# Staging the first feed-forward's results in the attention output's buffer, and a written order for ScalarE and VectorE in two of its four blocks

## Chip, cores and metric

One core of one Trainium2 chip. The metric is the device time of one execution in microseconds (us), and lower is better. The kernel before takes 912.31 us, the median of three runs (911.75 to 914.02).

## The reference, cut to what matters

```python
def reference(**kwargs):
    attn_out = _attn_ref(...)            # banded local attention plus 32 global tokens, 4 x 8 heads of 64
    B, H, S, D = attn_out.shape          # 4, 8, 544, 64
    x = attn_out.transpose(0, 2, 1, 3).reshape(B * S, H * D)     # 2176 tokens x 512
    x = _moe_ref(x, w_in, w_out)         # elu(x @ w_in) @ w_out, width 2048
    return _moe2_ref(x, w_gate, w_val, w_out, rms_g)
    # rms norm; silu(xn @ w_gate) * (xn @ w_val) @ w_out, width 1536
```

The weights arrive as 64-bit floats and are decoded on the chip to 32-bit ones with integer instructions. Every product of two 32-bit numbers is made of three passes over a high and a low part.

## The kernel before, in words

**First half, to about 500 us.** The 2048 local tokens go through the first feed-forward in four blocks of 512, called b=0 to b=3 here as in the code (so the change's "blocks 2 and 3" are b=1 and b=2). A block has 16 turns j. In a turn TensorE makes one `mm1` (12 matmuls L132 into `h`), then `mm2` of the turn before (12 matmuls L146 into the four accumulators `y0` to `y3`, in two halves), and between them pieces of the attention of block b+1: scores (L220, L226) at turns 0, 4, 8, 12, transposes (`ptp`, L244) one turn later, the product with v (`o`, L257) after the `mm1` of the turn after that. At turn 15 the attention's output `x` is transposed into `xT` for the next block (L280 to L282). The last `mm2` of a block comes in turn 0 of the next one, and `store_y` (L152 to L160) then evicts `y0` to `y3`, two on ScalarE and two on VectorE, and sends them to `yT` in DRAM with four DMAs of 256 KB.

Between `mm1` and `mm2` stands the elu: ScalarE `e<-h` (L121), ScalarE exp (L122), VectorE `e<-e,h` (L123), ScalarE `g<-e` (L139), VectorE low part `g<-e,g` (L140). The `e` tiles have two buffers, and two of the four eviction tiles `yev` take the same two; the other two take the two buffers `stg`.

**Weight decoding beside it.** In b=0 the first feed-forward's own weights are decoded; from turn 13 of b=0 on, through b=1 and b=2, the second one's (24 tasks: 18 decodings and 6 sums). A decoding is ScalarE |raw| (L83), four VectorE instructions (L90 to L93), then DMAs of the result to DRAM (`wS`, `wT`) and the load of the next 1 MB of raw weights into the raw buffer that came free. There are two raw buffers and two `dx` buffers. The sums (`w2_sums`, L483 to L486) are made in the raw buffer itself, so the load after them waits for their eight DMAs. SyncE issues all DMAs, in its own order.

TensorE's order is written out by hand throughout. ScalarE's and VectorE's is written by hand only in the first stretch of the kernel; in the rest a scheduler that plans with its own times chooses it. Tile pools hand out buffers by tag: a new tile of a tag waits until the readers of the one before it are done, DMAs among them. The tag `x32` has one buffer; the attention output `x` uses it from turn 2 to turn 15 of each block, in b=3 the global attention's `xg32`, and later a block of `yT` that is read back.

**Second half.** At turns 10 to 15 of b=3 the global tokens' first feed-forward runs beside the block; its result `yg` is copied (`ysb`, a `stg` tile), transposed (L721), evicted and stored. Then the second feed-forward's products follow: pairs of `product` (L732) into `A` and `Q`, ScalarE copies of `A` (L921, L936, L942), VectorE sums, and the second matmul `o` (L738), with ScalarE and VectorE splitting the weights (L586, L587) and squaring the next tokens (L609, L614) beside it.

Of the kernel before, what the change touches and what calls it, by code (L numbers as in the profile page):

```python
# [7 lines left out]
F32 = mybir.dt.float32  # L8
F32R = mybir.dt.float32r
# [3 lines left out]
AF = mybir.ActivationFunctionType  # L13
ALU = mybir.AluOpType
# [7 lines left out]
P = 128  # L22
# [6 lines left out]
HI_MIN = 2.0 ** -15  # L29
HI_MAX = 122880.0 - 2.0 ** -7  # L30
# [3 lines left out]
def f(ap):  # L34
    return ap.bitcast(F32)


def i32(ap):
    return ap.bitcast(I32)
# [3 lines left out]
def fused_kernel(ctx: ExitStack, tc: tile.TileContext, kq, vl, gkq, gv, w_in, w_out, w_gate, w_val, w_o2, rms_g, consts, out):  # L43
    nc = tc.nc
# [5 lines left out]
    stg = ctx.enter_context(tc.tile_pool(name="stg", bufs=2))  # L50
# [85 lines left out]
    def act1(h, n, fn=None):  # L136
        e = (fn or elu)(h, n)
        g = moe.tile([P, 2, 512], F32R, tag="g", name="g", bufs=2)
        nc.scalar.copy(g[:, 0, :n], e[:, :n])  # L139
        nc.vector.tensor_tensor(out=g[:, 1, :n], in0=e[:, :n], in1=f(g[:, 0, :n]), op=ALU.subtract)  # L140
        return g
# [8 lines left out]
        return [yps.tile([P, 512], F32, tag=f"y{i}", name=f"y{i}") for i in range(4)]  # L150

    def store_y(ys, t0, n):  # L152
        for dc in range(4):
            if dc % 2:
                t = moe.tile([P, 512], F32, tag="e", name="yev", bufs=2)
                nc.vector.tensor_copy(t[:, :n], ys[dc][:, :n])
            else:
                t = stg.tile([P, 512], F32, tag="stg", name="yev")
                nc.scalar.copy(t[:, :n], ys[dc][:, :n])
            nc.sync.dma_start(out=yT[:, dc, t0:t0 + n], in_=t[:, :n])  # L160


    SETS = ("A11", "A12", "S2", "S1", "S3", "A22", "S4")
# [14 lines left out]
    with ExitStack() as ls:  # L178
# [282 lines left out]
        def w2_decode(i):  # L461
            kind, c, G = order2[i]
            raw = raws2.pop(0)
            t = dec_abs(dec["t"], raw, keep=True)
            dec_bits(t, raw)
            t2 = t.rearrange("p (a n) -> p a n", a=2)
            if kind == "o":
                nc.sync.dma_start(out=wT[c:c + 2].rearrange("a p n -> p a n"), in_=t2)
                w2_load()
            elif c == 0:  # L470
                put(kind, G, "A11", t2[:, :, 0:256])
                held["a"] = t2
                w2_load()
            else:
                put(kind, G, "A12", t2[:, :, 0:256])
                put(kind, G, "A22", t2[:, :, 256:512])
                held["b"], held["raw"] = t2, raw

        def w2_sums(kind, G):
# [4 lines left out]
            nc.vector.tensor_tensor(out=s2, in0=s1, in1=t[:, :, 0:256], op=ALU.subtract)  # L484
            nc.vector.tensor_tensor(out=s3, in0=t[:, :, 0:256], in1=t[:, :, 256:512], op=ALU.subtract)
            nc.vector.tensor_tensor(out=s4, in0=u[:, :, 0:256], in1=s2, op=ALU.subtract)  # L486
            for name, src in (("S2", s2), ("S1", s1), ("S3", s3), ("S4", s4)):
                put(kind, G, name, src)
            w2_load()

        tasks = []
        for G in range(3):
            for kind in "gv":
                tasks += [("d", kind, 0, G), ("d", kind, 2, G), ("s", kind, G)]
            tasks += [("d", "o", 4 * G, 0), ("d", "o", 4 * G + 2, 0)]

        def w2_task():
            if tasks:
                what, *of = tasks.pop(0)
                if what == "d":  # L500
                    w2_decode(order2.index(tuple(of)))
                else:
                    w2_sums(*of)

        def slot0(j, part, h):
            g = act1(h, 512, elu_a) if part == 0 else None
# [11 lines left out]
        moe_block(0, slot0)  # L518


        def slot12(b):
            def slot(j, part, h):
                g = act1(h, 512, elu_a) if part == 0 else None
                att_slot(b, j, part)
                if part == 2 and j % 4 != 3:
                    w2_task()
                return g

            return slot

        for b in (1, 2):
            moe_block(b, slot12(b))
        assert not tasks


# [182 lines left out]
    def g_finish(ysb):  # L718
        pt = aps.tile([P, 512], F32, tag="att", name="ygt")
        for i in range(4):  # L720
            nc.tensor.transpose(pt[:, i * P:(i + 1) * P], ysb[:, i * P:(i + 1) * P], ident)  # L721
        yt = stg.tile([P, 512], F32, tag="stg", name="yev")
        nc.scalar.copy(yt, pt)
        nc.sync.dma_start(out=yT[:, :, 16 * P:17 * P], in_=yt.rearrange("p (c t) -> p c t", c=4))

    def product(ps, k, i, pos, m, first=True):
        n, q = sizes[k], 14 * i + 2 * pos + m
# [48 lines left out]
    xg = xgp.tile([P, 4, 2, P], F32R, name="xg")  # L776
    with ExitStack() as gs:
        gp = gs.enter_context(tc.tile_pool(name="gp", bufs=1))
        xg32 = moe.tile([P, 4, 512], F32, tag="x32", name="xg32")
        zero = gp.tile([P, 64], F32, name="zero")[:, 0:1]  # L780
        nc.vector.memset(zero, 0.0)
        G = {}
# [64 lines left out]
        def g_X(u):  # L847
            d = G.pop(u)
            b, par = u // 2, u % 2
            x = aps.tile([P, P], F32, tag="att", name="gx")  # L850
            nc.tensor.transpose(x[:64, :], d["e"], ident)
            nc.scalar.copy(xg32[64 * par:64 * par + 64, :, b * 32:b * 32 + 32], x[:64, :].rearrange("d (a q) -> d a q", a=4))

        def slot3(j, part, h):
            g = act1(h, 512) if part == 0 else None
            b = j // 2
            if j < 8:
                if j % 2 == 0:
                    if part < 2:
                        g_S(b, part)  # L860
                    elif b:
                        g_PV(2 * b - 1)
                        g_load_v(2 * b + 1)
                        g_X(2 * b - 2)
                elif part < 2:
                    g_T(2 * b + part)
                else:
                    g_load_k(b + 1)
                    g_PV(2 * b)
                    g_load_v(2 * b + 2)  # L870
                    if b:
                        g_X(2 * b - 1)
            elif j == 8 and part == 2:
                g_PV(7)
                g_X(6)
            elif j == 9 and part == 0:
                g_X(7)
                nc.scalar.copy(xg[:, :, 0, :], xg32[:, :, :P])
                nc.vector.tensor_tensor(out=xg[:, :, 1, :], in0=xg32[:, :, :P], in1=f(xg[:, :, 0, :]), op=ALU.subtract)
            elif j == 9 and part == 2:  # L880
                gs.close()
                second_start()
            if j >= 10:
                if part == 0:
                    if 0 <= j - 11 < 4:
                        gg[j - 11] = g_act(gg.pop("e"))
                    if j - 12 < 3:
                        second_mm2(j - 12)
                    second_mm1(j - 10)
                if part == 2:  # L890
                    second_slot(j - 10)
            return g
# [180 lines left out]
```

## Time and profile before

| what | value |
|---|---|
| median of the runs | 912.31 us (911.75, 912.31, 914.02) |
| profiled execution, its own time | 914.21 us |
| profiled execution, span | 912.30 us |
| TensorE busy | 870.9 us, 95% of the span |
| VectorE busy | 587.0 us, 64% |
| ScalarE busy | 476.0 us, 52% |
| granted clock, mean | 0.983 |

The span is the time from the first to the last instruction; 1.9 us of the execution lie outside it. TensorE is busy 95% of it. To read the profile, find in the slices the few stretches where TensorE is not busy, look up the granted clock there, and ask of each stretch which wait ended last.

### The profile page before, as it was taken

What the parts mean: (1) busy time and instruction counts of PE and PEld (TensorE: products, weight loads), DVE (VectorE), ACT (ScalarE), POOL (GpSimd) and SP (SyncE); (2) the same over time, 40 slices, a digit from 0 to 9 for tenths busy, and PEclk for the clock granted to TensorE, in tenths of its full rate; (3) what the DMA queues carried; (4) which work ended last, traced back from release to release, by engine and by line L of the source; (5) the groups of instructions that cost most, each with busy time, mean ns of one, the idle gap of its engine ahead of it and who ended that gap; (6) DMA issues with size and microseconds to landing.
All of it is one profiled execution on the core that took longest, in us unless ns stands there. A gap on an engine that the chain in (4) does not pass through costs nothing.

```text
span 912.3 us, 16268 instructions
## 1 busy us (share of the span) xinstructions
PE 870.9 (95%) x6652; PEld 741.3 (81%) x6652; DVE 587.0 (64%) x983; ACT 476.0 (52%) x863; POOL 18.5 (2%) x22
## 2 busy tenths in 40 slices
PE   4789999899999999999999799999999999999996
PEld 3567877688887888777888699997999998899985
DVE  4899978667678763543489455886355786365642
ACT  4677664345454544333456456665445665355531
POOL 0000000000000000000110100000100100000000
PEclk8999999899999999999999899999999999999999
DMA  9785365766686862351405532243122333133200
GB/s 361 279 300 203 124 239 176 260 206 220 223 300 216 256 198 110 128 191 59 165 1 184 172 94 93 93 136 118 58 93 93 113 98 102 52 123 116 93 24 35
DMA packets 60370, 139.27 MB, mean 153 GB/s; under 512 B 5000, under 2 KB 30728, under 8 KB 57736
## 3 DMA queue, kind: packets, MB, share of 16 engines
q1 hardware_dynamic: 60296, 138.24, 44.0%
q8 instruction: 52, 0.85, 0.4%
q14 instruction: 22, 0.18, 0.1%
HBM read 115.15 MB, written 23.07 MB: 152 GB/s over the span
## 4 chain that ended last, share of the span: by engine, by line
PE 75%; DVE 10%; DMA 8%; ACT 3%; issue 2%; SPq 1%; ACTq 0%; DVEq 0%
PE A L732 16%; PE o L738 15%; PE y L146 13%; PE h L132 13%; PE Q L732 11%; DMA yT<-yev 2%; DMA kq<-in_kq 2%; DMA raw<-in_moe_w_in 2%; DVE dx L92 2%; DVE dx L93 1%; PE o L257 1%; PE ptp L244 1%; DVE dx L90 1%; PE s L226 1%; PE hg L667 1%
## 5 line engine op out<-in xcount | busy, mean ns | idle before, releaser
L146 PE MATMUL y<-g,wA 128*128 128x512 f32 x768 | 200.5, 404 | 7.0 <-DVE g L140 5.2
L132 PE MATMUL h<-xT,wA 128*128 128x512 f32 x768 | 186.9, 392 | 1.7 <-DVE xT L282 1.7
L146 PEld LDWEIGHTS y<-g,wA 128*128 128x128 f32 x768 | 141.6, 191 | 43.8 <-DVE g L140 8.2
L132 PEld LDWEIGHTS h<-xT,wA 128*128 128x128 f32 x768 | 143.9, 189 | 32.9 <-DVE xT L282 2.4
L732 PE MATMUL A<-xc,wS 128*128 128x384 f32 (+1 forms) x864 | 156.8, 330 | 0.0
L732 PEld LDWEIGHTS A<-xc,wS 128*128 128x128 f32 x864 | 146.5, 189 | 3.9
L738 PE MATMUL o<-wB,p 128*128 128x512 f32 x612 | 147.4, 392 | 0.8 <-ACT p L742 0.3
L738 PEld LDWEIGHTS o<-wB,p 128*128 128x128 f32 x612 | 113.6, 188 | 24.8 <-DVE p L743 2.4
L732 PE MATMUL Q<-xc,wS 128*128 128x384 f32 (+1 forms) x648 | 115.3, 326 | 0.0
L732 PEld LDWEIGHTS Q<-xc,wS 128*128 128x128 f32 x648 | 107.8, 188 | 0.0
L587 DVE TENSOR_TENSOR wS<-wraw,wS 128x1024 fp32r<-128x1024 f32 x63 | 77.7, 1233 | 36.6 <-ACT wS L586 36.5
L747 DVE TENSOR_TENSOR t<-t,Q 128x384 f32<-128x384 f32 (+1 forms) x108 | 55.8, 527 | 39.4 <-PE Q L732 28.9
L586 ACT CAST wS<-wraw 128x1024 fp32r<-128x1024 f32 x63 | 65.9, 1050 | 18.8 <-PE Q L732 11.9
L139 ACT CAST g<-e 128x512 fp32r<-128x512 f32 x64 | 39.8, 622 | 53.7 <-DVE e L123 37.2
L121 ACT ACTIVATE e<-h 128x512 f32<-128x512 f32 x48 | 29.0, 605 | 72.1 <-PE h L132 63.6
L123 DVE SCALAR_TENSOR_TENSOR e<-e,h 128x512 f32<-128x512 f32 x48 | 32.5, 678 | 40.7 <-ACT e L122 40.7
L140 DVE TENSOR_TENSOR g<-e,g 128x512 fp32r<-128x512 f32 x64 | 43.7, 683 | 9.1 <-ACT g L139 8.8
L743 DVE TENSOR_TENSOR p<-p,p 128x384 fp32r<-128x384 f32 x36 | 19.9, 556 | 43.3 <-ACT p L742 43.3
L83 ACT ACTIVATE dx<-raw 128x1024 f32<-128x1024 f32 x34 | 39.3, 1158 | 16.2 <-DMA raw<-in_moe_w_gate 5.5
L90 DVE TENSOR_SCALAR dx<-dx 128x1024 f32<-128x1024 f32 x34 | 23.3, 689 | 34.2 <-ACT dx L83 34.0
L238 ACT ACTIVATE E<-s,mx 128x128 f32<-128x128 f32 x128 | 34.8, 385 | 17.1 <-DVE mx L236 17.1
L92 DVE SCALAR_TENSOR_TENSOR dx<-raw,dx 128x1024 int32<-128x1024 int32 x34 | 41.9, 1238 | 0.6
(173 smaller groups left out, 869.5 us busy)
## 6 DMA issues: line engine op xcount, KB each, us to landing
wraw<-wS SPq DMA_DIRECT2D x63, 512.0 KB, 3.3
raw<-in_moe_w_out SPq DMA_DIRECT2D x14, 1024.0 KB, 8.7
raw<-in_moe_w_in SPq DMA_DIRECT2D x8, 1024.0 KB, 6.2
raw<-in_moe_w_gate SPq DMA_DIRECT2D x6, 1024.0 KB, 6.1
raw<-in_moe_w_val SPq DMA_DIRECT2D x6, 1024.0 KB, 6.8
wS<-raw SPq DMA_DIRECT2D x48, 128.0 KB, 2.6
gvr<-in_gv SPq DMA_DIRECT2D x8, 640.0 KB, 4.0
wS<-dx SPq DMA_DIRECT2D x36, 128.0 KB, 2.1
```

What stands on the lines that cost most here:

```text
L83: ins = nc.scalar.activation(x, f(words(raw)[:, :, 1]), AF.Abs)
L92: nc.vector.scalar_tensor_tensor(out=i32(x), in0=word[:, :, 1], scalar=-0x40000000, in1=i32(x), op0=ALU.bitwise_and, op1=ALU.bitwise_or)
L132: nc.tensor.matmul(h[:, :n], W1[c, G][:, ws, o:o + P], xT[c][:, xs, :n], start=(k == 0), stop=(k == 11))
L139: nc.scalar.copy(g[:, 0, :n], e[:, :n])
L140: nc.vector.tensor_tensor(out=g[:, 1, :n], in0=e[:, :n], in1=f(g[:, 0, :n]), op=ALU.subtract)
L146: nc.tensor.matmul(ys[dc][:, :n], W2[j][:, ws, dc * P:(dc + 1) * P], g[:, gs, :n], start=(j == 0 and k == 0), stop=(j == 15 and k == 2))
L238: nc.scalar.activation(e[par][:, pr, :], ss[par][:, pr, :], AF.Exp, bias=mx[:, par, pr:pr + 1], scale=SCALE)
L586: nc.scalar.copy(t[:, :, 0, :], raw)
L587: nc.vector.tensor_tensor(out=t[:, :, 1, :], in0=raw, in1=f(t[:, :, 0, :]), op=ALU.subtract)
L732: nc.tensor.matmul(ps[:, :n], w[:, 2 * (q % 4) + c, ws, :], x[:, c, xs, :n], start=(first and c == 0 and z == 0), stop=(c == 1 and z == 2) ...
L738: nc.tensor.matmul(o, p[:, pp, t * P:(t + 1) * P], Wo[j][:, ww, :], start=(first and z == 0), stop=(last and z == 2))
L747: nc.vector.tensor_tensor(out=t, in0=t, in1=ps, op=ALU.add)
```

## The change

It does three things.

`store_y` puts the four evictions of b=0, 1 and 2 into one tile of tag `x32`, and sends it with a single DMA of 1 MB. For b=3 it stays as it was. `xg32` is therefore taken only when it is first written.

In b=1 and b=2 ScalarE and VectorE keep the order of the code. There a decoding is a generator: its |raw| is issued at the end of a turn (`w2_begin`), its VectorE instructions in pieces around the next turn's elu, and the rest at that turn's end, with the DMAs. In turn 15 the elu is spread over the turn's three parts.

The copy of `yg` goes into a tile of tag `xT3` instead of `stg`, and stands ahead of the last `mm2` and `store_y` of b=3; the eviction after its transposes goes into the second half of the same tile.

```diff
     def store_y(ys, t0, n):
+        t = moe.tile([P, 4, 512], F32, tag="x32", name="yev") if t0 < 1536 else None
         for dc in range(4):
+            if t is not None:
+                o = t[:, dc]
...
+        if t is not None:
+            nc.sync.dma_start(out=yT[:, :, t0:t0 + n], in_=t)
...
+        def w2_begin():
+            if not tasks:
+                return iter(())
+            what, *of = tasks.pop(0)
+            if what == "s":
+                return w2_sums(*of)
+            raw = raws2.pop(0)
+            return w2_bits(order2.index(tuple(of)), raw, dec_abs(dec["t"], raw, keep=True))
...
             def slot(j, part, h):
+                if part == 0:
...
+                    nc.scalar.activation(e, h, AF.Relu, scale=-1.0)
+                    if j < 15:
+                        nc.scalar.activation(e, e, AF.Exp, scale=-1.0)
+                        next(now[0], None)
+                        nc.vector.scalar_tensor_tensor(out=e, in0=e, scalar=-1.0, in1=h, op0=ALU.add, op1=ALU.max)
+                        nc.scalar.copy(g[:, 0, :], e)
+                        next(now[0], None)
+                        nc.vector.tensor_tensor(out=g[:, 1, :], in0=e, in1=f(g[:, 0, :]), op=ALU.subtract)
...
                 att_slot(b, j, part)
...
+                if part == 2:
+                    for _ in now[0]:
+                        pass
+                    now[0] = w2_begin() if j % 4 != 2 else iter(())
...
-        for b in (1, 2):
-            moe_block(b, slot12(b))
+        with tc.manual_schedule(engines={mybir.EngineType.DVE, mybir.EngineType.Activation}):
+            now[0] = w2_begin()
+            for b in (1, 2):
+                moe_block(b, slot12(b))
...
         second_mm2(3)
+        ysb = moe.tile([P, 2, 512], F32, tag="xT3", name="ysb")
+        nc.vector.tensor_copy(ysb[:, 0], gg["y"])
         finish_block()
-    ysb = stg.tile([P, 512], F32, tag="stg", name="ysb")
-    nc.vector.tensor_copy(ysb, gg["y"])
```

What this does to the engines' programs, at three places. First ScalarE from the elu of turn 0 of b=1 to that of turn 1: `y_733` and `y_735` are the accumulators of b=0, `E` the attention's exponentials, `ET` the evicted transposes. Before:

```order
L139 CAST g<-e 128x512
L159 COPY yev<-y_733 128x512
L238 ACTIVATE E<-s,mx 128x128 x8
L159 COPY yev<-y_735 128x512
L83 ACTIVATE dx<-raw 128x1024
L121 ACTIVATE e<-h 128x512
L246 COPY ET<-ptp 128x512
L122 ACTIVATE e<-e 128x512
L246 COPY ET<-ptp 128x512
L83 ACTIVATE dx<-raw 128x1024
```

And in the changed kernel, the same stretch:

```order
L554 CAST g<-e 128x512
L246 ACTIVATE E<-s,mx 128x128 x8
L164 COPY yev<-y_733 128x512
L164 COPY yev<-y_735 128x512
L83 ACTIVATE dx<-raw 128x1024
L549 ACTIVATE e<-h 128x512
L551 ACTIVATE e<-e 128x512
L554 CAST g<-e 128x512
L254 COPY ET<-ptp 128x512 x2
L549 ACTIVATE e<-h 128x512
```

Both evictions now come behind all eight exponentials. The L83 that stands here is that of the next task, one later than the L83 in the same place before; the elu of turn 1 and the two `ET` copies stand behind it.

Second ScalarE from the `ET` copies of turn 1 of b=2 to the elu of turn 2. Before:

```order
L246 COPY ET<-ptp 128x512 x2
L83 ACTIVATE dx<-raw 128x1024
L139 CAST g<-e 128x512
L121 ACTIVATE e<-h 128x512
L122 ACTIVATE e<-e 128x512
L139 CAST g<-e 128x512
L83 ACTIVATE dx<-raw 128x1024
```

And changed:

```order
L554 CAST g<-e 128x512
L254 COPY ET<-ptp 128x512 x2
L83 ACTIVATE dx<-raw 128x1024
L549 ACTIVATE e<-h 128x512
L551 ACTIVATE e<-e 128x512
L554 CAST g<-e 128x512
```

The last L83 of both is the decoding of the same weights (the third task of the block); it stood behind turn 2's elu and now stands ahead of it.

Third VectorE from the last elu of b=3 into the second half (`ysb` is the copy of the global tokens' result, `yev` the evictions of b=3). Before:

```order
L140 TENSOR_TENSOR g<-e,g 128x512
L587 TENSOR_TENSOR wB<-wraw,wB 128x2x512 x2
L156 COPY yev<-y_4195 128x512
L156 COPY yev<-y_4197 128x512
L587 TENSOR_TENSOR wS<-wraw,wS 128x8x128
L901 COPY ysb<-yg 128x512
```

And changed:

```order
L140 TENSOR_TENSOR g<-e,g 128x512
L635 TENSOR_TENSOR wB<-wraw,wB 128x2x512 x2
L950 COPY ysb<-yg 128x512
L162 COPY yev<-y_4179 128x512
L162 COPY yev<-y_4181 128x512
L635 TENSOR_TENSOR wS<-wraw,wS 128x8x128
```

The copy moved ahead of both evictions and one weight split.

TensorE's program is the same, matmul for matmul. SyncE's stays the same but for the stores themselves and a few neighbours that change places.

## Rows read from the trace of the kernel before

**Rows 1.** The page's busy tenths in 40 slices of 22.8 us, TensorE.

```profile
PE   4789999899999999999999799999999999999996
```

**Rows 2.** Windows: stretch; busy us of PE, PEld, DVE, ACT, POOL; clock, DMA, GB/s.

```profile
160.00:180.00 20.00, 17.16 (x124) 13.30 (x123) 13.06 (x22) 7.34 (x13) 0.00 (x0) 0.83 0.74 252
```

**Rows 3.** Timeline, b=1 turns 1 to 3: start, us, engine, line, what [idle before <-releaser].

```profile
164.77 2.88 PE L132 MATMUL h<-xT,wA 128*128 128x512 f32 x12
...
167.84 0.60 ACT L121 ACTIVATE e<-h 128x512 f32<-128x512 f32 x1 [6.00 <-DMA yT<-yev]
...
168.96 0.67 PE L257 MATMUL o<-v__1726,ET 128*32 128x65 f32 x32 [1.31 <-ACT ET L246]
...
172.62 5.06 PE L146 MATMUL y<-g,wA 128*128 128x512 f32 x11 [0.18 <-DVE g L140]
...
177.48 3.24 PE L132 MATMUL h<-xT,wA 128*128 128x512 f32 x12
```

**Rows 4.** Timeline, the same two `mm1` in undisturbed turns 6 and 7 of b=1.

```profile
196.68 2.88 PE L132 MATMUL h<-xT,wA 128*128 128x512 f32 x12
...
203.38 2.88 PE L132 MATMUL h<-xT,wA 128*128 128x512 f32 x12
```

**Rows 5.** A weight load's issue (timeline); landings (DMA view, us last); last store (chain).

```profile
158.57 0.37 SPq L75 DMA_DIRECT2D raw<-in_moe_w_val  x1
...
raw<-in_moe_w_val SPq DMA_DIRECT2D x1, 1024.0 KB, 5.3
...
kq__1905<-in_kq SPq DMA_DIRECT2D x1, 704.0 KB, 7.5
...
161.28 7.49 DMA yT<-yev
```

**Rows 6.** Busiest groups of the page: xcount | busy us, mean ns | idle before.

```profile
L139 ACT CAST g<-e 128x512 fp32r<-128x512 f32 x64 | 39.8, 622 | 53.7 <-DVE e L123 37.2
...
L83 ACT ACTIVATE dx<-raw 128x1024 f32<-128x1024 f32 x34 | 39.3, 1158 | 16.2 <-DMA raw<-in_moe_w_gate 5.5
...
L238 ACT ACTIVATE E<-s,mx 128x128 f32<-128x128 f32 x128 | 34.8, 385 | 17.1 <-DVE mx L236 17.1
L92 DVE SCALAR_TENSOR_TENSOR dx<-raw,dx 128x1024 int32<-128x1024 int32 x34 | 41.9, 1238 | 0.6
```

**Rows 7.** Timeline, b=2 turns 0 to 3.

```profile
265.90 0.69 DVE L123 SCALAR_TENSOR_TENSOR e<-e,h 128x512 f32<-128x512 f32 x1 [3.55 <-ACT e L122]
...
271.47 1.53 PE L146 MATMUL y<-g,wA 128*128 128x512 f32 x6
...
275.09 2.88 PE L132 MATMUL h<-xT,wA 128*128 128x512 f32 x12
...
280.39 2.76 PE L146 MATMUL y<-g,wA 128*128 128x512 f32 x11 [0.94 <-DVE g L140]
...
283.00 2.88 PE L132 MATMUL h<-xT,wA 128*128 128x512 f32 x12
```

**Rows 8.** Timeline, from the first half to the second.

```profile
499.38 2.35 DVE L587 TENSOR_TENSOR wB<-wraw,wB 128x1024 fp32r<-128x1024 f32 x2
...
508.06 0.69 DVE L901 COPY ysb<-yg 128x512 f32<-128x512 f32 x1 [3.07 <-DMA yT<-yev]
...
508.89 1.09 PE L721 MATMUL ygt<-ident,ysb 128*128 128x128 f32 x4 [6.25 <-DVE ysb L901]
...
513.38 0.48 ACT L921 COPY t<-A 128x384 f32<-128x384 f32 x1 [0.96 <-PE A L732]
...
518.16 0.52 ACT L742 CAST p<-t 128x384 fp32r<-128x384 f32 x1
...
519.42 2.24 PE L732 MATMUL A<-xc,wS 128*128 128x384 f32 x12
...
521.50 2.24 PE L738 MATMUL o<-wB,p 128*128 128x512 f32 x9
```

**Rows 9.** DMA view, one raw weight load of b=1 issued behind others.

```profile
raw<-in_moe_w_gate SPq DMA_DIRECT2D x1, 1024.0 KB, 10.4
```

More of the change, by code (lines that the diff above doesn't have):

```diff
@@ L152, in store_y @@
     def store_y(ys, t0, n):
+        t = moe.tile([P, 4, 512], F32, tag="x32", name="yev") if t0 < 1536 else None
         for dc in range(4):
+            if t is not None:
+                o = t[:, dc]
+            elif dc % 2:
+                o = moe.tile([P, 512], F32, tag="e", name="yev", bufs=2)
+            else:
+                o = stg.tile([P, 512], F32, tag="stg", name="yev")
             if dc % 2:
-                t = moe.tile([P, 512], F32, tag="e", name="yev", bufs=2)
-                nc.vector.tensor_copy(t[:, :n], ys[dc][:, :n])
-            else:
-                t = stg.tile([P, 512], F32, tag="stg", name="yev")
-                nc.scalar.copy(t[:, :n], ys[dc][:, :n])
-            nc.sync.dma_start(out=yT[:, dc, t0:t0 + n], in_=t[:, :n])
+                nc.vector.tensor_copy(o, ys[dc])
+            else:
+                nc.scalar.copy(o, ys[dc])
+            if t is None:
+                nc.sync.dma_start(out=yT[:, dc, t0:t0 + n], in_=o)
+        if t is not None:
+            nc.sync.dma_start(out=yT[:, :, t0:t0 + n], in_=t)
     SETS = ("A11", "A12", "S2", "S1", "S3", "A22", "S4")
@@ L495, in fused_kernel @@
             tasks += [("d", "o", 4 * G, 0), ("d", "o", 4 * G + 2, 0)]
-        def w2_task():
[L498 to L503, printed above, removed]
+        def w2_begin():
[6 more added lines that the diff above has]
+            return w2_bits(order2.index(tuple(of)), raw, dec_abs(dec["t"], raw, keep=True))
+        def w2_task():
+            for _ in w2_begin():
+                pass
         def slot0(j, part, h):
@@ L518, in fused_kernel @@
         moe_block(0, slot0)
+        now = [iter(())]
         def slot12(b):
+            hold = {}
             def slot(j, part, h):
-                g = act1(h, 512, elu_a) if part == 0 else None
-                att_slot(b, j, part)
-                if part == 2 and j % 4 != 3:
-                    w2_task()
-                return g
-            return slot
-        for b in (1, 2):
-            moe_block(b, slot12(b))
+                if part == 0:
+                    e = moe.tile([P, 512], F32, tag="e", name="e", bufs=2)
+                    g = moe.tile([P, 2, 512], F32R, tag="g", name="g", bufs=2)
+                    nc.scalar.activation(e, h, AF.Relu, scale=-1.0)
[6 more added lines that the diff above has]
+                        nc.vector.tensor_tensor(out=g[:, 1, :], in0=e, in1=f(g[:, 0, :]), op=ALU.subtract)
+                    else:
+                        hold["e"], hold["g"], hold["h"] = e, g, h
+                    att_slot(b, j, part)
+                    return g
+                att_slot(b, j, part)
+                if j == 15:
+                    e, g = hold["e"], hold["g"]
+                    if part == 1:
+                        nc.scalar.activation(e, e, AF.Exp, scale=-1.0)
+                        nc.vector.scalar_tensor_tensor(out=e, in0=e, scalar=-1.0, in1=hold["h"], op0=ALU.add, op1=ALU.max)
+                    else:
+                        nc.scalar.copy(g[:, 0, :], e)
+                        nc.vector.tensor_tensor(out=g[:, 1, :], in0=e, in1=f(g[:, 0, :]), op=ALU.subtract)
+                if part == 2:
+                    for _ in now[0]:
+                        pass
+                    now[0] = w2_begin() if j % 4 != 2 else iter(())
+            return slot
+        with tc.manual_schedule(engines={mybir.EngineType.DVE, mybir.EngineType.Activation}):
+            now[0] = w2_begin()
+            for b in (1, 2):
+                moe_block(b, slot12(b))
         assert not tasks
@@ L720, in g_finish @@
         for i in range(4):
[L721 to L724, printed above, removed]
+            nc.tensor.transpose(pt[:, i * P:(i + 1) * P], ysb[:, 0, i * P:(i + 1) * P], ident)
+        nc.scalar.copy(ysb[:, 1], pt)
+        nc.sync.dma_start(out=yT[:, :, 16 * P:17 * P], in_=ysb[:, 1].rearrange("p (c t) -> p c t", c=4))
     def product(ps, k, i, pos, m, first=True):
@@ L778, in fused_kernel @@
         gp = gs.enter_context(tc.tile_pool(name="gp", bufs=1))
-        xg32 = moe.tile([P, 4, 512], F32, tag="x32", name="xg32")
         zero = gp.tile([P, 64], F32, name="zero")[:, 0:1]
@@ L849, in g_X @@
             b, par = u // 2, u % 2
+            if u == 0:
+                G["x"] = moe.tile([P, 4, 512], F32, tag="x32", name="xg32")
+            xg32 = G["x"]
             x = aps.tile([P, P], F32, tag="att", name="gx")
@@ L877, in slot3 @@
                 g_X(7)
+                xg32 = G["x"]
                 nc.scalar.copy(xg[:, :, 0, :], xg32[:, :, :P])
```

14 lines of the change are left out of this document (10 added, 4 removed).

## Prediction

> **What bounds the kernel now.** I first read the busy slices [rows 1]. TensorE shows 9 almost everywhere; after the opening only two slices fall to 7, and a window over the first shows the granted clock down at 0.83 [rows 2]. So TensorE is the bound, and only those holes, and smaller ones like them, can be closed. Next I read the timeline in each hole for the wait that ended last.
>
> The first hole is the start of b=1 [rows 3]. ScalarE's elu of turn 1 waited 6.00 us for `yT<-yev`: its `e` buffer still held an eviction that was being stored. The `ET` copies stood behind it, `o` waited 1.31 us for them, and then the turn's `mm2` waited for g. When it came, 11 matmuls took 5.06 us, about 460 ns each: the lower level (1.2 GHz) after those pauses. From the `mm1` of turn 2 to that of turn 3 it is 177.48 - 164.77 = 12.7 us; the same distance undisturbed is 203.38 - 196.68 = 6.7 [rows 4]. That is 6.0 lost, and 0.4 more since the next `mm1` is still slow (3.24 against 2.88): 6.4 us. The start of b=2 has the same shape, milder and at the full clock: 283.00 - 275.09 = 7.9 against 6.7, 1.2 us lost [rows 7].
>
> The second hole is the end of the first half [rows 8]. The `ysb` copy waited until 508.06 for a store out of its `stg` buffer; the transposes stood 6.25 us behind it, and all products stand behind the transposes.
>
> **The change part by part.** *The staging at the start of b=1.* The `x32` buffer is free from turn 15 to turn 2 of the next block, so the evictions no longer take `e` or `stg`, and the 6.00 us wait has no cause left. What is late next? Two things, both from the written order. First, both `y0` and `y2` are now evicted behind all eight exponentials. I work this out at b=2, where the chain begins at 265.90 [rows 7]; short VectorE steps that follow one another start 0.60 apart there. The elu step 0.65, a decoding piece 1.24 [rows 6], the low part 0.60, the first maximum with its scaling 0.8: exponentials from 269.2, eight at 0.27 apart (2.2; 385 ns each, overlapping [rows 6]) to 271.4, the eviction of `y0` to 272.05. TensorE wants that bank at 271.47 [rows 7]: 0.6 lost, in b=1 as well. Second, the next task's |raw| now stands ahead of the elu of turn 1. Its weights are issued at 158.57 and land 5.3 later, at 163.9 [rows 5]. |raw| 1.16 [rows 6], the two activations 1.25, the elu step 0.7, the cast 0.62 [rows 6]: g's high part at 167.6, the first `ET` at 168.2. `o` is wanted at 164.77 + 2.72 + 0.6 = 168.1 (a `mm1` takes 2.72 when the next follows at once). About 0.3 us is lost here. Gain at b=1: 6.4 - 0.9 = 5.5 us, with no pause left that would lower the clock.
>
> The next holder of `x32`, the attention output, is first written at turn 2, on VectorE behind that turn's elu (about 173.8 in the same count). The one store is issued when the last eviction is done, 162.2; with the 7.49 us of the last of the four stores [rows 5] it lands near 170. If it didn't, the whole of VectorE's queue would stand; TensorE would miss it only one turn later. I cost this at nothing.
>
> *The start of b=2.* Here the same order costs more than it brings. The decoding of turn 0 ends behind the two VectorE evictions, at 272.5. SyncE then issues, in this order, the store (1024 KB), the decoded weights (512 KB) and the load for turn 2's task (1024 KB), 2560 KB from about 272.65. For the landing I have two points [rows 5]: 1024 KB alone in 5.3 us; and the load of 158.57, a 704 KB key load and the four stores, 2752 KB, complete at 161.28 + 7.49 = 168.8, 10.2 us after the first issue. Between them 2560 KB takes 9.7 us: the load lands at 282.3. ScalarE's |raw| waits for it, and behind it stands the elu of turn 2, whose h is ready at 278.4. From the landing: |raw| 1.16, activations 1.25, elu step 0.7, cast 0.62, so the high part comes at 286.1; the low part follows a decoding piece, at 287.35. TensorE wants g at 275.09 + 0.6 + 6.7 + 2.72 = 285.1. It waits 1.0, makes one matmul (0.23), and waits 1.0 again: 2.0 lost. With the eviction's 0.6 that is 2.6 against 1.2 before: 1.4 us worse.
>
> What a store and a load cost is where a page differs from the rows. The Trainium skill (DMA: Bandwidth & Descriptors, section Anatomy of one DMA) gives a transfer issued from GpSimd as about 2.0 us plus its bytes at 436 GB/s; by that the 2560 KB land after an estimated 8.0 us, the pause shrinks to some 0.4 us, and the sum below ends at 900.5. For 1024 KB the same formula gives 4.4 where the row shows 5.3 [rows 5]; I go by the row.
>
> *The other turns.* A turn without attention is 5.4 us of TensorE, and the elu's chain with one decoding piece is 3.8 us long, so a late |raw| is hidden up to about 1 to 2 us. Loads issued two turns ahead land in time. Three more are issued only one turn ahead (turn 6 of b=1, turns 6 and 10 of b=2). With 5.3 to 7 us to land I count the elu 1 to 2 us late there and TensorE not waiting, by margins of 0.9 to 1.3 us. Nothing taken, and a loss if a load is later; below nothing is excluded, since TensorE has no pauses there now. In turn 15 the elu is spread over three parts, but its g is wanted only in the next block's turn 0.
>
> *The copy of the global tokens' result.* The `xT3` tile is free when `mm1` of the last turn is done, so the copy runs behind the two weight splits, 499.38 + 2.35 = 501.7 [rows 8], and ends at 502.4, as the last `mm2` ends. Transposes to 503.0, products from there: TensorE pauses no more. But `stg` still has its store. The tile of the squares (`acc`, L609) is now the next one to take that buffer, and stands in ScalarE's order between the copies of the two first `A` products. It waits for the landing that released `ysb` before, just under 508.06 [rows 8]. From the second copy to the end of the cast `p` it was 518.16 + 0.52 - 513.38 = 5.3 us [rows 8]; now from 508.6, so to 513.9. The third pair of products, a pair being 2.08 (521.50 - 519.42) [rows 8], may write `A` only when the copy ahead of that cast is done, 513.35, and `o` follows at 515.4. It started at 521.50 [rows 8]: 6.1 us gained. If the squares didn't hold ScalarE, five pairs from 503.0 would bring `o` at 513.4, 8.1 gained; the lower bound is the transposes' wait moved into ScalarE entirely, about 4. I take 6.1, since the wait it rests on is in a row.
>
> *Sum.* 912.3 (span) - 5.5 + 1.4 - 6.1 = 902.1, a gain of 10.2 us. The profiled execution took 914.21, 1.9 more than its span; the median of the runs, 912.31, happens to equal the span. From the median the forecast is 912.3 - 10.2 = 902.1.
>
> **The rivals.** *The loads land in time.* If the three transfers at b=2 overlap better than my line, and the squares hold ScalarE for less, the two new pauses go: 902.1 - 2.0 - 2.0 = 898.1. For it: the 5.3 us of [rows 5] was measured with two others behind it.
>
> *The clock falls at b=2.* Two pauses of 1 us with one matmul between look like those of [rows 3], where it fell; at 280 a single 0.94 us [rows 7] didn't lower it. Price from [rows 3]: 5.06 for 11 matmuls instead of 2.5, and 0.4 after: 2.9 us, 905.0.
>
> *The wait at b=1 only changes its name.* If the load of 158.57 lands as late as the store beside it, near 168.8, |raw| holds the elu of turn 1 as long as the store did: the 5.5 us are not gained, 907.6. That is also how the change would fail to do what it says. Against it: the 5.3 us is a measured landing of that very load, and its issue is unchanged.
>
> *Written order makes the loads the bound (slower).* ScalarE can no longer pass over a |raw| whose weights are out. One load of b=1 that was issued behind others took 10.4 us [rows 9], 5.1 more than I count. If all five loads issued one turn ahead did, TensorE would lose 5 x 5.1 less margins of 0 + 1.3 + 0 + 0.9 + 0.9, 22.4 us: 924.5. It eats the whole gain once each is later by (10.2 + 3.1) / 5 = 2.7 us. Against it: elsewhere in b=1 and b=2 such loads had fewer transfers ahead of them.
>
> **How the numbers follow.** The forecast has 0.46, loads in time 0.2, the clock 0.15, the renamed wait 0.1, the slower one 0.09. Range: 897.5 leaves out little of the first rival, 909 takes in the next two with 1.4 to spare for small pauses in other turns; the slower rival stays outside. A measurement of this kernel can tell about 0.3% (2.7 us) from no change: faster means below 909.6. The first three cases and most of the fourth lie there: 0.86. Same 0.06, from the rest of the fourth and a slower rival in small. Slower 0.08.
>
> **What would show it.** Right: no `e<-h` waiting for `yT<-yev` any more; the slice at 160 to 180 us at full clock; the distance of the two `mm1` at b=1 near 7.6; a |raw| at turn 1 to 2 of b=2 waiting about 5 us for its raw load with TensorE idle for two pauses of 1 us behind it; the transposes L721 of old right behind the last `mm2`; `acc` waiting for `yT<-yev`, and some 2 us of TensorE waits on ScalarE copies before the first `o`. Wrong: TensorE waits on g in turns 6 or 10, a clock below 1 in b=1 or b=2, or `x` on VectorE waiting for the store.

## The result, and the profile after

The changed kernel takes 902.86 us (median of six runs, 901.44 to 905.01) against 912.03 of the kernel before beside it (911.60 to 914.16): a ratio of 0.9894, 95% interval 0.9878 to 0.9911, 9.2 us faster. The forecast was 902.1 in a range of 897.5 to 909. The profiled execution of the changed kernel took 902.84 us with a span of 901.0.

TensorE's busy tenths in 40 slices, from the page of the changed kernel, and below them windows as in [rows 2]: the opening of b=1 and the crossing into the second half in the changed kernel, and last the crossing in the kernel before.

```profile
PE   4789999999999999999999999999999999999997
...
160.00:180.00 20.00, 19.74 (x163) 15.51 (x169) 14.10 (x23) 10.19 (x18) 0.00 (x0) 1.00 0.98 322
500.00:520.00 20.00, 18.11 (x98) 16.73 (x97) 11.03 (x15) 12.59 (x23) 3.85 (x3) 1.00 0.49 169
...
500.00:520.00 20.00, 13.75 (x68) 13.01 (x67) 8.39 (x11) 9.97 (x18) 3.03 (x3) 0.83 0.54 177
```

The two low slices of [rows 1], an 8 and a 7, are 9s now. From 160 to 180 us TensorE is busy for 19.74 us instead of 17.16, at a granted clock of 1.00 instead of 0.83 [rows 2]. The crossing ran at 0.83 before, too.

The opening of b=1, from the timeline, which answers to [rows 3]:

```profile
160.81 1.66 PE L146 MATMUL y<-g,wA 128*128 128x512 f32 x6 [0.26 <-ACT yev L164]
...
162.59 1.15 ACT L83 ACTIVATE dx<-raw 128x1024 f32<-128x1024 f32 x1 [1.35 <-DMA raw<-in_moe_w_val]
163.64 0.58 ACT L549 ACTIVATE e<-h 128x512 f32<-128x512 f32 x1
...
164.57 2.90 PE L132 MATMUL h<-xT,wA 128*128 128x512 f32 x12
167.41 1.12 PE L265 MATMUL o<-v__1726,ET 128*32 128x65 f32 x64
168.45 3.00 PE L146 MATMUL y<-g,wA 128*128 128x512 f32 x12
171.29 2.88 PE L132 MATMUL h<-xT,wA 128*128 128x512 f32 x12
```

The elu of turn 1 no longer waits for a store, `o` and `mm2` follow without a pause, and from one `mm1` to the next it is 171.29 - 164.57 = 6.72 us, as in undisturbed turns [rows 4]. What is left is a wait for an eviction, 0.26 us by its bracket (the number in square brackets, the idle time before an instruction).

The opening of b=2, which answers to [rows 7]; SPq lines are DMA issues:

```profile
265.48 1.66 PE L146 MATMUL y<-g,wA 128*128 128x512 f32 x6 [0.27 <-ACT yev L164]
...
265.94 0.55 SPq L168 DMA_DIRECT2D yT<-yev  x1
266.53 0.63 SPq L480 DMA_DIRECT2D wT<-dx  x1
267.21 1.07 SPq L75 DMA_DIRECT2D raw<-in_moe_w_gate  x1
...
275.58 1.12 ACT L83 ACTIVATE dx<-raw 128x1024 f32<-128x1024 f32 x1 [4.97 <-DMA raw<-in_moe_w_gate]
...
279.46 0.51 PE L146 MATMUL y<-g,wA 128*128 128x512 f32 x1 [0.64 <-ACT g L554]
280.54 2.79 PE L146 MATMUL y<-g,wA 128*128 128x512 f32 x11 [0.58 <-DVE g L556]
```

Here is the new loss: |raw| waits 4.97 us for its load, the elu of turn 2 stands behind it, and TensorE pauses twice, at the full clock.

The crossing into the second half, which answers to [rows 8]:

```profile
494.44 2.35 DVE L635 TENSOR_TENSOR wB<-wraw,wB 128x1024 fp32r<-128x1024 f32 x2
496.72 0.68 DVE L950 COPY ysb<-yg 128x512 f32<-128x512 f32 x1
497.45 0.66 PE L769 MATMUL ygt<-ident,ysb 128*128 128x128 f32 x4
...
503.54 0.52 ACT L657 ACTIVATE acc<-ya 128x384 f32<-128x384 f32 x1 [3.85 <-DMA yT<-yev]
...
504.49 1.32 PE L779 MATMUL A<-xc,wS 128*128 128x384 f32 x6 [1.15 <-ACT t L971]
...
508.46 2.38 PE L779 MATMUL A<-xc,wS 128*128 128x384 f32 x12 [0.56 <-ACT t L986]
510.68 2.25 PE L785 MATMUL o<-wB,p 128*128 128x512 f32 x9
```

The copy runs right behind the weight splits. The wait for the store, 6.25 us on TensorE's transposes before [rows 8], is now 3.85 us of ScalarE at `acc`, of which 1.15 and 0.56 reach TensorE. The rest of the gain is the clock: behind the 6.25 us, the first twelve products ran partly at the lower level (1.2 GHz) in the kernel before,

```profile
509.63 3.71 PE L732 MATMUL A<-xc,wS 128*128 128x384 f32 x12
```

and the same twelve take 2.35 us in the changed kernel. From the start of the transposes to the `Q` behind these products it was 513.18 - 508.89 = 4.29 us and is 500.06 - 497.45 = 2.61, 1.7 us less.

**One ruler for all kernels.** TensorE's program is the same in all of them, so I compare starts of the same matmuls. The first two columns are the times from the `mm1` of turn 0 to that of turn 4, the third from the last eleven matmuls of the last elu's `mm2` (494.42 before, 489.34 after) to the first `o`; all in us, from each kernel's one trace.

| kernel | b=1 | b=2 | crossing | median of the runs |
|---|---|---|---|---|
| before | 32.69 | 26.75 | 27.08 | 912.03 |
| after | 26.94 | 27.92 | 21.34 | 902.86 |
| `y_only` | 32.56 | 25.55 | 22.84 | 907.51 |
| `s_only` | 26.34 | 25.58 | 26.83 | 905.75 |
| `o_only` | 28.82 | 26.13 | 27.20 | 910.17 |
| `sy` | 26.33 | 25.57 | 21.99 | 901.37 |
| `late_abs` | 26.90 | 26.14 | 20.84 | 901.48 |
| `free_acc` | 26.89 | 27.97 | 18.93 | 900.99 |
| `both` | 26.94 | 26.13 | 18.90 | 898.55 |
| `sy_free` | 26.34 | 25.58 | 18.98 | 897.35 |

From before to after: -5.75, +1.17 and -5.74, together -10.3. The spans differ by 11.3: the changed kernel also reached b=1 0.80 us earlier (149.79 against 150.59), ahead of the first place that the change is about; over all traces that time goes from 148.74 to 151.25. The medians differ by 9.2; the profiled execution of before, 914.21, lies 2.2 above its median. In each row of the table the three places together gain 0.6 to 2.4 us more against this one trace than the medians do. So the places tell where time went, and the medians how much.

### The profile page after: what moved, and what is told of

Read it like the earlier page. It is cut to its first block, busy times and chain, and to the rows that moved or that the text cites. A ratio compares the mean times of both kernels' runs of the same rounds, so it can differ in the third digit from the quotient of the medians.

```text
span 901.0 us, 16261 instructions
## 1 busy us (share of the span) xinstructions
PE 868.2 (96%) x6652; PEld 738.2 (82%) x6652; DVE 591.6 (66%) x983; ACT 476.1 (53%) x863; POOL 19.4 (2%) x22
## 4 chain that ended last, share of the span: by engine, by line
PE 77%; DVE 12%; DMA 4%; ACT 4%; issue 2%; SPq 1%; POOL 0%; ACTq 0%
PE A L779 15%; PE y L146 15%; PE o L785 14%; PE h L132 13%; PE Q L779 11%; DMA kq<-in_kq 2%; PE s L234 1%; DVE dx L92 1%; ACT E L246 1%; PE o L265 1%; DVE dx L93 1%; PE ptp L252 1%; DMA raw<-in_moe_w_gate 1%; DVE wA L99 1%; PE hg L715 1%
## 5 line engine op out<-in xcount | busy, mean ns | idle before, releaser
L83 ACT ACTIVATE dx<-raw 128x1024 f32<-128x1024 f32 x34 | 39.2, 1156 | 26.4 <-DMA raw<-in_moe_w_gate 7.2
L549 ACT ACTIVATE e<-h 128x512 f32<-128x512 f32 x32 | 19.4, 605 | 42.6 <-PE h L132 42.5
L789 ACT CAST p<-p 128x384 fp32r<-128x384 f32 x36 | 18.5, 514 | 41.6 <-PE o L785 41.4
L553 DVE SCALAR_TENSOR_TENSOR e<-e,h 128x512 f32<-128x512 f32 x30 | 20.5, 685 | 26.7 <-ACT e L551 26.7
L663 POOL TENSOR_TENSOR acc<-acc,sq 128x384 f32<-128x384 f32 (+1 forms) x18 | 19.1, 1064 | 680.9 <-ACT sq L662 495.9
```

Source lines behind the costliest of these rows:

```text
L553: nc.vector.scalar_tensor_tensor(out=e, in0=e, scalar=-1.0, in1=h, op0=ALU.add, op1=ALU.max)
```

## The experiments

Theory: three places account for the difference, b=1 by the staging, the crossing by the early copy, and the start of b=2 as a price of the written order. Rivals: the written order brings part of the gain, or the loads that it waits for are the next bound.

### Each part alone

`y_only` is the kernel before with the early copy:

```diff
+        ysb = moe.tile([P, 2, 512], F32, tag="xT3", name="ysb")
+        nc.vector.tensor_copy(ysb[:, 0], gg["y"])
         finish_block()
-    ysb = stg.tile([P, 512], F32, tag="stg", name="ysb")
...
```

> The kernel before with one of the three parts: the copy of the global tokens' result in the xT3 tile, ahead of the last mm2 and its evictions. My theory, each part acts at its own place: the first o of the second half comes 5.9 us earlier and nothing else changes, so 906 us where before has 912; the squares' acc still waits for the evictions' store. Rival, the place is bound by something else (weight splits or the clock): under 3 us, 909 or more.

`s_only` is the kernel before with the staging in `x32`:

```diff
+        t = moe.tile([P, 4, 512], F32, tag="x32", name="yev") if t0 < 1536 else None
...
+        if t is not None:
+            nc.sync.dma_start(out=yT[:, :, t0:t0 + n], in_=t)
```

> The kernel before with one part: the evictions of b=0 to 2 in the x32 tile and one store; ScalarE's and VectorE's order as the scheduler makes it. My theory, the waits at the starts of b=1 and b=2 were the e buffers held by stores: the two mm1 distances fall to 6.7 us at both places, a gain of 6.4 and 1.2 us, 904.4. Rival, the written order is what makes the start of b=1 run through: the distance at b=1 stays above 9 us, total 908 to 912.

`o_only` is the kernel before with the written order and the decoding in pieces (`slot12` as in the change; four stores out of `e` and `stg` as before):

```diff
...
+        with tc.manual_schedule(engines={mybir.EngineType.DVE, mybir.EngineType.Activation}):
+            now[0] = w2_begin()
+            for b in (1, 2):
+                moe_block(b, slot12(b))
```

> The kernel before with one part: the written order and the decoding in pieces in b=1 and b=2; evictions stay in e and stg with four stores. My theory, order alone takes away no wait: the elu of turn 1 still waits for the store, and now all of ScalarE stands behind it and behind the raw loads; the mm1 distance at b=1 stays at 11 to 14 us, that of b=2 grows to 9 to 11, total 912 to 916. Rival, the order is the gain: 905 to 909, with no elu waiting for yT.

`sy` is the changed kernel without that, staging and copy alone:

```diff
...
-        with tc.manual_schedule(engines={mybir.EngineType.DVE, mybir.EngineType.Activation}):
-            now[0] = w2_begin()
-            for b in (1, 2):
-                moe_block(b, slot12(b))
+        for b in (1, 2):
+            moe_block(b, slot12(b))
```

> The changed kernel with its order undone: staging and the result's copy, but ScalarE and VectorE in the scheduler's order. My theory: 6.4 + 1.2 + 5.9 us gained, 898.5, which is 2 to 4 us faster than the changed kernel, since the pauses of 1.2 us at b=2 and of 0.3 us at both evictions come from the written order. Rival, the order is needed: 904 or more.

| kernel | median (range), runs | ratio to before, 95% interval |
|---|---|---|
| `y_only` | 907.51 (906.41 to 908.18), 5 | 0.9948 [0.9932, 0.9964] |
| `s_only` | 905.75 (904.97 to 906.29), 4 | 0.9933 [0.9910, 0.9956] |
| `o_only` | 910.17 (908.55 to 911.15), 10 | 0.9976 [0.9965, 0.9987] |
| `sy` | 901.37 (901.01 to 901.59), 4 | 0.9882 [0.9863, 0.9901] |

Before had 912.26 us beside them. Copy and staging add: 4.75 and 6.51 give 11.3, `sy` has 10.9. On top of them the written order costs 1.5 us (901.37 to 902.86); the intervals of the two ratios overlap, so the medians alone do not settle it. The places say where: without it b=2 is undisturbed (25.57 for 27.92), b=1 0.6 shorter and the crossing 0.65 longer. In `sy` the |raw| of b=2 waits for its load too, but behind the elu of turn 2, so that only turn 3 could miss it (timeline of `sy`):

```profile
274.18 0.62 ACT L139 CAST g<-e 128x512 fp32r<-128x512 f32 x1 [1.10 <-DVE e L123]
276.73 1.12 ACT L83 ACTIVATE dx<-raw 128x1024 f32<-128x1024 f32 x1 [1.93 <-DMA raw<-in_moe_w_gate]
278.51 0.60 ACT L121 ACTIVATE e<-h 128x512 f32<-128x512 f32 x1 [0.66 <-PE h L132]
```

After that wait ScalarE is still idle for 0.66 us before the next h.

Three of the four were slower than expected: `y_only` by 1.5 us, `s_only` by 1.4 and `sy` by 2.9. For `s_only` the places gave what was expected, 7.8 us against 7.6; by the medians it is 6.5. In `y_only` the first `o` came 4.2 us earlier and not 5.9, since the wait at `acc` reached TensorE for 2.11 us in one piece and the products behind it ran partly at the lower level (2.83 us for twelve where 2.24 is full speed).

`o_only` missed its expectation of 912 to 916: alone, the order makes the kernel 2.1 us faster, for it eases the same wait that the staging removes. Timeline of `o_only`, the opening of b=1:

```profile
167.52 0.60 ACT L541 ACTIVATE e<-h 128x512 f32<-128x512 f32 x1 [2.12 <-DMA yT<-yev]
...
169.53 0.62 ACT L546 CAST g<-e 128x512 fp32r<-128x512 f32 x1 [0.75 <-DVE e L545]
170.06 1.07 ACT L246 COPY ET<-ptp 128x512 f32<-128x512 f32 x2
...
170.69 1.16 PE L257 MATMUL o<-v__1726,ET 128*32 128x65 f32 x64 [1.79 <-ACT ET L246]
171.78 3.02 PE L146 MATMUL y<-g,wA 128*128 128x512 f32 x12
```

The elu still waits for a store, until about the same time as before [rows 3]. But its cast stands ahead of the `ET` copies, so when `o` can start, g is there too: one pause of 1.79 us in place of four (1.31, 0.34, 1.00 and 0.18), and 12 matmuls in 3.02 us, at the full clock, where 11 took 5.06 [rows 3]. So order and staging share one gain at b=1: 3.87 us with the order alone, 6.35 with the staging alone, no more than that with both (5.75 in the changed kernel).

At b=2 the order alone costs nothing (26.13 against 26.75), although its |raw| stands in the same place. Its four stores are issued one by one from 267.45, 5.1 us ahead of the `mm1` of turn 2 (272.58), and |raw| starts at 276.60, 4.0 behind that `mm1`. In the changed kernel the single store must wait for all four evictions: it is issued 3.3 us ahead of that `mm1` (265.94, 269.24), and |raw| starts 6.3 behind it. So the pauses at b=2 need both parts, the single store and the order. In `y_only` too, b=2 is 1.2 us shorter than before, though that edit touches nothing there: the 0.94 us pause of [rows 7] comes and goes. Against a b=2 without that pause (25.57 in `sy`) the changed kernel loses 2.35 us there, not 1.17.

### What the order costs at b=2, and what the accumulator costs

`late_abs` moves |raw| of the five loads issued one turn ahead behind part 1 of the next turn's slot, and so behind that turn's elu:

```diff
+                if part == 1 and pend[0]:
+                    pend[0] = False
+                    now[0] = w2_begin()
...
-                    now[0] = w2_begin() if j % 4 != 2 else iter(())
+                    now[0] = iter(())
+                    if j % 4 != 2:
+                        pend[0] = bool(tasks) and tasks[0] in LATE
+                        if not pend[0]:
+                            now[0] = w2_begin()
```

> The changed kernel, but of the five raw loads that are issued one turn ahead, the decoding's first ScalarE step (|raw|) is issued after the block's slot work of part 1 instead of before it, so that a late load no longer holds up the exponentials and casts written behind it. Theory (the two pauses of 0.64 and 0.58 us at b=2 come from |raw| waiting 4.97 us for a load with the exponentials behind it): pauses 0 at b=2, the first mm1 of turn 4 some 1.2 us earlier, time 901.5 us (901 to 902.5). Rival (the order itself, not the place of |raw|, costs TensorE the time that the kernel without the written order saves): pauses move to another instruction, time 902.5 to 903.5.

`free_acc` takes the two `stg` eviction tiles of b=3 and the last transposed tile from other buffers, so that `acc` has no store in front of it:

```diff
-                o = stg.tile([P, 512], F32, tag="stg", name="yev")
+                o = bpools["gg"].tile([P, 512], F32, tag="sq", name="yev")
...
-        nc.scalar.copy(ysb[:, 1], pt)
+        yt = bpools["gg"].tile([P, 2, 512], F32, tag="gg", name="yt")[:, 0]
+        nc.scalar.copy(yt, pt)
```

> The changed kernel, with block 3's two ScalarE eviction tiles of the first feed-forward and the last transposed tile taken from the buffers of the gate activations, so that the first accumulator of the second part no longer stands behind a store of yT. Theory (after the change the last wait at the third place is the accumulator's 3.85 us for that store, which delays a copy for TensorE by 1.15 us and an activation by 0.56 us): no wait of ScalarE for yT there, the first o some 1.7 us earlier, time 901.1 us (900.5 to 901.8). Rival (the casts and the reload of wraw are late next, in place of the accumulator): 902.3 to 903.3.

`both` has the two edits together.

> The two edits before this one together, on the changed kernel. Theory: the places are far apart on one TensorE queue, so the gains add: 1.2 and 1.7 off 902.9, 900.0 us (899.3 to 901). Rival (one gain is given back later, by a weight load that isn't there earlier): no faster than the better of the two alone.

`sy_free` is `sy` with the second edit.

> The kernel with the two staging edits and without the written order, plus the freed accumulator (eviction tiles and the last transposed tile in the gate activations' buffers). Theory (order and accumulator are apart, the accumulator's wait costs this kernel 1.90 and 0.58 us on TensorE at the third place): 901.4 less 2.3, 899.1 us (898.3 to 900), the same as the changed kernel with both edits, 898.6, within 0.3%. Rival (the written order, once its late loads hold nothing up, brings something of its own): 900.5 or more, above 898.6 by over 0.2%.

| kernel | median (range), runs | ratio to before, 95% interval |
|---|---|---|
| `late_abs` | 901.48 (900.23 to 901.90), 4 | 0.9886 [0.9869, 0.9903] |
| `free_acc` | 900.99 (899.60 to 902.40), 4 | 0.9883 [0.9864, 0.9902] |
| `both` | 898.55 (897.24 to 899.02), 4 | 0.9853 [0.9833, 0.9873] |
| `sy_free` | 897.35 (896.61 to 898.53), 4 | 0.9837 [0.9822, 0.9851] |

Before had 911.71 beside the first three and 912.36 beside the last. In `late_abs` TensorE has no pause after the eviction's at b=2, though |raw| still waits:

```profile
277.16 1.13 ACT L83 ACTIVATE dx<-raw 128x1024 f32<-128x1024 f32 x1 [0.97 <-DMA raw<-in_moe_w_gate]
```

b=2 is 1.78 us shorter, the crossing 0.50, the median 1.4 (the intervals of this kernel and of the changed one overlap, as do those of `free_acc`; that of `both` lies apart). In `free_acc` `acc` has run before the crossing, at 488.52, ScalarE goes straight from the copy of the last transposes to the squares (timeline), and the first `o` comes 2.4 us earlier; the median falls by 1.9:

```profile
499.56 0.58 ACT L771 COPY yt<-ygt 128x512 f32<-128x512 f32 x1
500.04 0.94 ACT L662 ACTIVATE sq<-ya 128x384 f32<-128x384 f32 x2
```

The gains add in `both` by the places, 4.2 us; by the medians it is 4.3, more than 1.4 and 1.9 together, and `both` and `sy_free` came out 0.8 and 1.0 us below their expected ranges. `sy_free` has the lowest time of all, 897.35. It and `both` are not told apart by their intervals; the places differ by 0.6 at b=1 and at b=2, the two evictions behind the exponentials. So nothing here shows a gain from the written order once the other two waits are gone.

### Late loads

`slow_loads` is the changed kernel with 1 MB of extra DMA ahead of each of the five loads issued one turn ahead; `sy_slow_loads` and `late_slow` are `sy` and `late_abs` with the same:

```diff
+            if src is not None and n_raw2[0] in (3, 6, 13, 15, 17):
+                for i in range(1 if n_raw2[0] % 2 and n_raw2[0] != 13 else 2):
+                    junk = dram.tile(list(src.shape), F32, name=f"junk{n_raw2[0]}_{i}")
+                    nc.sync.dma_start(out=junk, in_=src)
```

> The changed kernel with 1 MB of extra DMA queued ahead of each of the five raw loads that are issued one turn ahead, which makes each some 2.9 us later by the load rows (7.5 less 5.3 us for 704 KB more, scaled to 1024). This prices the rival by which the written order makes the loads the bound. By the rival's formula (every lateness above the margins 0, 1.3, 0, 0.9, 0.9 lands on TensorE, five waits): 5 x 2.9 less 3.1, 914.3 us (910 to 917). Other theory (each late load costs only what is left after the matmuls queued ahead of the waiting exponential, and about a turn of 5.6 us of them is there): 904 to 907.

> The kernel with the two staging edits and without the written order, with the same 1 MB of extra DMA ahead of the same five raw loads. If the written order is what makes late loads dear (with it they cost 922.0 less 902.9 = 19.1 us): a third of that or less, 901.4 plus 3 to 6, 904.5 to 907.5 us. If the loads are dear under either order, since in both an |raw| with a late load stands ahead of exponentials on ScalarE's queue: 915 to 921 us.

> The changed kernel with |raw| of the five loads behind the slot's work of part 1, and the same 1 MB of extra DMA ahead of each of the five. If it is the place of |raw| on ScalarE's queue that makes a late load dear: most of the 19.1 us goes, as a load has the half turn of 2.9 us more before it holds an exponential, 901.5 plus 2 to 6, 903.5 to 907.5 us. If it is the DMA traffic or the later steps of the decoding (casts, planes) that are late: within 3 us of 922.

| kernel | median (range), runs | ratio to before, 95% interval | against itself without the extra DMA |
|---|---|---|---|
| `slow_loads` | 922.02 (920.17 to 924.17), 4 | 1.0114 [1.0089, 1.0140] | +19.2 |
| `sy_slow_loads` | 904.17 (903.18 to 907.95), 4 | 0.9918 [0.9894, 0.9942] | +2.8 |
| `late_slow` | 904.01 (902.65 to 905.99), 4 | 0.9904 [0.9887, 0.9920] | +2.5 |

Before had 911.71 us beside the first and 912.36 beside the other two. `slow_loads` is dearer than either theory said. Timeline of it at turns 2 and 3 of b=2, and at turn 6 and turn 10:

```profile
284.35 1.12 ACT L83 ACTIVATE dx<-raw 128x1024 f32<-128x1024 f32 x1 [7.39 <-DMA raw<-in_moe_w_gate]
...
288.22 0.51 PE L146 MATMUL y<-g,wA 128*128 128x512 f32 x1 [3.08 <-ACT g L558]
289.31 4.27 PE L146 MATMUL y<-g,wA 128*128 128x512 f32 x11 [0.58 <-DVE g L560]
...
318.45 0.51 PE L146 MATMUL y<-g,wA 128*128 128x512 f32 x1 [1.90 <-ACT g L558]
319.54 2.79 PE L146 MATMUL y<-g,wA 128*128 128x512 f32 x11 [0.58 <-DVE g L560]
...
346.45 0.50 PE L146 MATMUL y<-g,wA 128*128 128x512 f32 x1 [1.27 <-ACT g L558]
347.54 4.38 PE L146 MATMUL y<-g,wA 128*128 128x512 f32 x11 [0.59 <-DVE g L560]
```

The five |raw| wait 3.7, 3.9, 2.4, 3.0 and 3.6 us longer than in the changed kernel (for example 7.39 against 4.97), 16.5 in all, 3.3 each. (The expectation's own rows give 3.2 each, 2.2 us scaled from 704 to 1024 KB, not its 2.9.) By `mm1` starts the five stretches grow by 4.90, 2.47, 3.89, 3.13 and 4.01 us, 18.4 in all. With the prediction's margins, 16.5 - 3.1 = 13.4 was due. The rest is the clock: in three of the five stretches the matmuls behind the pause ran partly at the lower level (4.27 and 4.38 us for eleven, where 2.79 is full speed, and 4.60 for twelve at b=1, where 3.00 is), some 4.7 us. So in the sum the rival's formula held for the waits, and left out the clock.

With the same extra DMA, `late_slow` loses 2.5 us and `sy_slow_loads` 2.8, a little less than expected. In the trace of `late_slow` four of the five stretches take what they take in `late_abs`, to 0.2 us, so it isn't the traffic: it is the |raw| that stands in front of an elu. One elu later in ScalarE's queue, 3 us of lateness cost nothing at these four. At the fifth, b=1 (31.04 for 26.90), the late decoding does cost: ScalarE has the exponential ready in time, but VectorE's step of the elu stands behind the pieces of the decoding, and TensorE waits for it; the eleven matmuls behind that pause take 4.31 us, partly at the lower level.

```profile
169.59 0.64 ACT L557 ACTIVATE e<-e 128x512 f32<-128x512 f32 x1
...
173.81 0.69 DVE L500 TENSOR_TENSOR raw<-raw,dx 128x512 f32<-128x512 f32 x1
174.41 0.68 DVE L559 SCALAR_TENSOR_TENSOR e<-e,h 128x512 f32<-128x512 f32 x1
...
175.80 0.50 PE L146 MATMUL y<-g,wA 128*128 128x512 f32 x1 [1.82 <-ACT g L560]
```

That trace is of the slowest of the four executions, 905.99. For `sy_slow_loads` it stays open how much is the queue as it was and how much the scheduler, which saw the extra DMAs and may have planned around them.

## Why the prediction was right, step by step

- **The staging at b=1**: forecast -5.5, measured -5.75. The wait had no cause left, and no pause remained to lower the clock. The eviction behind the exponentials was put at 0.6 and took 0.56 by `mm1` starts (6.91 us from turn 1 to turn 2, 6.35 in `sy_free`). The 0.3 us for |raw| did not come: its load, issued at 157.67, landed 4.9 us later and not 5.3, and `ET` was done when `o` wanted it. By the prediction's own times, 168.2 against 168.1, it was 0.1 and not 0.3. The sign "the distance of the two `mm1` at b=1 near 7.6" missed: it is 6.72. That number has both losses in the one distance; the 0.3 did not come, and the eviction's 0.56 falls one turn earlier.
- **The start of b=2**: forecast +1.4, measured +1.17, or 2.35 where 2.6 was forecast if the pause of [rows 7] is left out on both sides. The landing was put at 9.7 us after the store's issue, by a line between two rows; it took 275.58 - 265.94 = 9.64. By the formula of the Trainium skill (DMA: Bandwidth & Descriptors, section Anatomy of one DMA), which is for one transfer issued from GpSimd, these bytes take an estimated 8.0; three transfers issued from SyncE took 1.6 us more here. The two pauses, put at 2.0, cost 7.23 - 5.44 = 1.79 from turn 3 to turn 4. They are recorded as 0.64 and 0.58: TensorE's bars overlap by 0.16 when nothing waits (168.45 + 3.00 against 171.29), so a pause costs more than its bracket says.
- **The other turns**: forecast 0, measured 0 to 0.1 (from turn 4 to turn 8 the changed kernel takes 25.58 us in b=1 and 25.66 in b=2, `sy` 25.57 in b=2). The store landed in time: `x` was written at 172.54 without a wait.
- **The crossing**: forecast -6.1, measured -5.74. The mechanism was the one written down, `acc` waiting for the store; the pauses at the copies before the first `o`, 1.15 and 0.56, are the "some 2 us" of the text. The prediction looked up the clock only in the first hole. Here it was 0.83 as well; the 1.7 us that this cost are inside the forecast 6.1 unnamed, since its rows begin behind the slow products, at 513.38. The upper end, 8.1 without that wait, is 8.15 in `free_acc`, 27.08 - 18.93.
- **The rivals.** That the loads land in time did not happen, but `both` reached that rival's 898.1 to within half a microsecond by taking the waits away. The clock stayed at 1.00 in b=1 and b=2 (windows 150 to 255 and 255 to 362 us). The wait at b=1 did not change its name. The slower rival did not happen, but the experiment shows it was well founded: at 3.3 us per load the waits cost what its formula says, in the sum, and the clock adds 4.7. Whether the gain is gone at 2.7 us per load, as it says, is not shown, since only one lateness was run.
- **What was wrong beside the sum**: I costed the written order as a price only. Alone it gains at b=1, as `o_only` shows; that a part's effect depends on what else is changed stood nowhere in the prediction. And the busy slices were misread: [rows 1] has an 8 and a 7 after the opening, not two 7s. The two holes are the right ones.

The sum, -10.2, was compared with spans (-11.3), places (-10.3) and medians (-9.2); it lies between them. The terms missed by -0.25, -0.23 and +0.36 us, which partly cancel; the scatter of one trace, about 1 to 2 us, is larger than each of them, so what the runs confirm is the mechanisms, and hits this close are in part luck.

## What to carry to other kernels

On an in-order engine that feeds TensorE, an instruction that waits for a DMA belongs behind the work that TensorE wants next; one elu later made 3 us of lateness free at four of five places here. At the fifth the work behind the late load held up VectorE's queue instead, so look at every engine that it passes through. Measure what a stall costs by the starts of the same matmuls in two traces, not by idle brackets, and price the lower clock with it. Before adding up the parts of a change, ask whether two of them remove the same wait.

## What the hardware showed that I had not expected

The length of a pause alone does not tell whether the granted clock falls behind it. It stayed up behind one pause of 1.79 us (`o_only`: 12 matmuls in 3.02 us) and behind 1.90 and 0.58 (`slow_loads`, eleven in 2.79), and fell behind 1.27 and 0.59 (eleven in 4.38). The nearest pair is in one trace: behind 1.31 and 0.58 at turn 6 of b=1 it stayed up,

```profile
204.91 0.51 PE L146 MATMUL y<-g,wA 128*128 128x512 f32 x1 [1.31 <-ACT g L558]
206.00 2.80 PE L146 MATMUL y<-g,wA 128*128 128x512 f32 x11 [0.58 <-DVE g L560]
```

and at turn 10 of b=2 almost the same pauses lowered it. The windows of `slow_loads` around turn 6 of b=1 and turns 2, 6 and 10 of b=2 show it; the clock is the third number from the end:

```profile
199.00:212.00 13.00, 11.10 (x69) 8.24 (x75) 8.57 (x16) 6.09 (x9) 0.00 (x0) 1.00 0.61 213
...
284.00:312.00 28.00, 24.34 (x227) 18.90 (x226) 17.75 (x30) 12.35 (x24) 0.00 (x0) 0.94 0.64 210
312.00:330.00 18.00, 15.52 (x133) 11.86 (x132) 12.25 (x24) 7.11 (x13) 0.00 (x0) 1.00 0.71 246
344.00:365.00 21.00, 19.14 (x145) 14.73 (x144) 11.34 (x22) 9.59 (x22) 0.00 (x0) 0.92 0.14 54
```

What else decides it is not settled by these runs.
